# Layer 2's first product with four pairs by seven half products on weights that layer 1 stored; layer 1's half tile sooner, input sums staggered, one step of a row later

## The chip, the core and the metric

The kernel runs on one core of one Trainium2 chip. The engines that matter are TensorE (PE, matmuls; its weight loads are PEld and overlap the matmuls), VectorE (DVE), ScalarE (ACT), GpSimd (POOL, little used here) and SyncE (SP), which only issues DMAs, in the order in which they stand in its queue. The metric is the device time of one execution in microseconds (us).

## The reference

The input x has 2048 tokens of 640 channels. Two layers are computed, each a spectral block and a block that mixes tokens:

```python
for _ in range(2):
    n = layernorm(x)                                   # over the 640 channels
    x = x + irfft2(rfft2(n) * (w_r + 1j * w_i))
    h = layernorm(x)
    u = gelu(h.T @ w1 + b1)                            # over tokens: [640, 2048] @ [2048, 1728]
    x = x + (u @ w2 + b2).T                            # [640, 1728] @ [1728, 2048]
```

Both layers use the same w1, b1, w2, b2, w_r and w_i. All is float32.

## The kernel before

**Stages.** `run` calls `a0_first`, then for each layer `a1` and `a2` (spectral block) and the MLP: `b1st` for layer 1, `b2nd` for layer 2. The instructions go through a small helper (`Pin`), so that the profile puts all of them on line 57; only DMA issues keep lines of their own.

**Products.** A float32 factor is split into two fp16 parts, a high and a low one (wh and wl for weights, hh and hl for the input of the MLP, uh and ul or u for its middle). A product then is three matmuls: high x high, high x low, low x high. The split of a weight tile needs its scale: ScalarE squares and sums the raw tile (`scan1`, written to `junk`), TensorE adds the partitions with `ones`, and VectorE makes a power of two (`scale1`). ScalarE then writes the high part, VectorE the low part (`wsplit`). Weights arrive by DMA in halves of 512 KB (`wload`, tiles named raw, S, or wh and wl where a free buffer of those serves).

**First product.** Its output has 14 tiles of 128 rows of F (the last holds 64 rows, and computes its two parts side by side, so that it takes 64 matmuls in place of 16 x 2 x 3 = 96). Each matmul has 320 columns. Layer 1 takes tiles 0 to 4 and the half tile (`L` = 13) whole (`plain`), and tiles 5 to 12 as four pairs (`PD` = 4). A pair is a 2 x 2 block product by Winograd's form: seven half products in place of eight, each of 8 x 3 = 24 matmuls of 320 columns. For it the weights are combined (`form`, S1 to S4) and split anew (`hi`, `lo`, tile wo), the input too, once for all pairs: `tsum`, `thi`, `tlo` make T1 to T4 of tiles k and k + 8 of the input, four sums and two parts for each k from 0 to 7. The seven results are added up in X (named uf in layer 1) by `evict`. Layer 2 takes all 14 tiles whole, 13 x 96 + 64 = 1312 matmuls.

**Second product.** Layer 1 computes 16 rows whole; while a row runs, the start of the next spectral block (`a0_fold1`, `a0_hi` with tile fh, `a0_lo` with tile fl, `s1_all`) is done for the row before it. Layer 2 takes eight pairs by seven half products of 21 matmuls.

**What sets the order.** In `b1st` the table `SIDE` says, as (tile, step): calls, what stands before step j of a whole tile; `FORM` and `DONE` do the same in `pairs`. In `b2nd` before, `ahead` and `prep` do it. Each engine and SP's queue run strictly in the order of the program; a DMA that waits holds up those behind it. With `pin` set the order is that of the code.

**Names the change touches.** In `b1st`: `SIDE`, `plain`, `hi`, `lo`, `pairs`, the second product's `held` and `s1_all`. In `b2nd`: all of its first product. `rawtile`, `wopen` and `wload` choose the buffers of the weights.

Of the kernel before, what the change touches and what calls it, by code (L numbers as in the profile page):

```python
# [20 lines left out]
SEQ = [t + 7 * i for t in (0, 6, 1, 2, 3, 4, 5) for i in range(2)]  # L21
# [13 lines left out]
M0, PD = 5, 4  # L35
LASTW = 24
# [104 lines left out]
class Layers:  # L141
# [51 lines left out]
    def setup(self):  # L193
# [29 lines left out]
        self.xs[0] = [A["x"][j] for j in range(NJ)]  # L223
        self.xs[4] = [A["out"][j] for j in range(NJ)]
# [435 lines left out]
    def a1(self, first):  # L660
# [317 lines left out]
    def a2(self, li):  # L978
# [6 lines left out]
        self.hf = [ph.tile([128, 2, 320], F32, name=f"hf{j}_{self.n}") for j in range(NJ)]  # L985
        p = self.push("a2", side=self.sq)

        xts = [p.tile([128, 642], F32, name=f"xt{i}_{self.n}") for i in range(5)]
        for q in xts:
            G.memset(q[:, D:], 0.0)  # L990
# [47 lines left out]
        for i in range(NJ + 3):  # L1038
# [60 lines left out]
    def wtile(self, m):  # L1099

        k, i = m // NFT, m % NFT if m < NFT else m - NFT
        if self.second:
            i = i // 2 + i % 2 * NQ if k else SEQ[i]
        return min(k, 1), i, NFT if k else NJ

    def rawtile(self, m, c):

        if not self.second and m in (8, 12):
            q = self.t(self.wp[1], [128, NJ, 128], F16, "wl" if c else "wh", 1)
# [18 lines left out]
    def wopen(self, m):  # L1128
        wh, wl = (self.t(self.wp[m % 2], [128, NJ, 128], F16, a, 1) for a in ("wh", "wl"))
# [29 lines left out]
    def b1st(self, li):  # L1159
# [9 lines left out]
        self.wsplit(1, hi=False)  # L1169
        self.wload(2)  # L1170
# [75 lines left out]
        def plain(ft):  # L1246
# [43 lines left out]
        s2, c2 = (self.base.tile([128, PD], F32, name=f"{a}1") for a in ("s2", "c2"))  # L1290

# [28 lines left out]
        def lo(n):  # L1320
# [3 lines left out]
            V.scalar_tensor_tensor(w[:, 1], src[n], s2[:, d:d + 1], w[:, 0], op0=ALU.mult, op1=ALU.subtract)  # L1324

# [43 lines left out]
        def pairs():  # L1369
            for n in range(NP + 1):  # L1370
# [16 lines left out]
                if not n:  # L1387
                    self.wload(a + 1)
# [10 lines left out]
                if i == 2 and not end:  # L1399
# [30 lines left out]
        for d in range(PD - 1):  # L1430
# [9 lines left out]
            (1, 1): [(tlo, 1)],  # L1440
            (2, 0): [(tsum, 2), (thi, 2), (self.wopen, 3), (self.scan1, L)], (2, 3): [(tlo, 2)],
            (2, 6): [(self.wsplit, 3, (0,))], (2, 8): [(self.wsplit, 3, (1,)), (self.wload, 6)],
            (2, 10): [(tsum, 3), (thi, 3)], (2, 13): [(tlo, 3)],
            (3, 0): [(tsum, 4), (thi, 4), (self.wopen, 4)], (3, 2): [(self.wsplit, 4, (0,))],
            (3, 4): [(self.wsplit, 4, (1,)), (self.wload, 7), (tlo, 4)], (3, 7): [(tsum, 5), (thi, 5)],
            (3, 6): [(self.scan1, 5)], (3, 11): [(tlo, 5)],
# [659 lines left out]
```

## Time and profile before

| | |
|---|---|
| time, median of 3 runs | 1002.23 us (1001.63 to 1249.45) |
| the profiled execution, its own time | 1001.94 us |
| its span | 1000.2 us |
| granted TensorE clock | 0.998 |
| TensorE busy | 963.3 us (96%), 8873 matmuls |
| VectorE busy | 731.3 us (73%) |
| ScalarE busy | 590.2 us (59%) |
| GpSimd busy | 253.9 us (25%) |
| SP's DMA queue | 134.35 MB, 40.7% of the 16 DMA engines |

The span runs from the first instruction to the last, and the execution's time adds what lies around it. In the views, `out<-in` names what an instruction writes and reads, `[0.66 <-DVE wo]` says that the engine was idle for 0.66 us until VectorE's write of wo released it, and x2 that two instructions stand in one row. In the views of windows each engine has its busy time in the window, and behind it the count of its instructions; the last three columns are the granted clock as a share of 2.4 GHz, the busy share of the 16 DMA engines and the bytes moved in GB/s. TensorE's matmuls overlap in their rows, so that a row's time is longer than the distance between two starts.

### The profile page before, as it was taken

What the parts mean: (1) busy time and instruction counts of PE and PEld (TensorE: products, weight loads), DVE (VectorE), ACT (ScalarE), POOL (GpSimd) and SP (SyncE); (2) the same over time, 40 slices, a digit from 0 to 9 for tenths busy, and PEclk for the clock granted to TensorE, in tenths of its full rate; (3) what the DMA queues carried; (4) which work ended last, traced back from release to release, by engine and by line L of the source; (5) the groups of instructions that cost most, each with busy time, mean ns of one, the idle gap of its engine ahead of it and who ended that gap; (6) DMA issues with size and microseconds to landing.
All of it is one profiled execution on the core that took longest, in us unless ns stands there. A gap on an engine that the chain in (4) does not pass through costs nothing. (4 is left out here: it accounts for less than half of the span.)

```text
span 1000.2 us, 21980 instructions
## 1 busy us (share of the span) xinstructions
PE 963.3 (96%) x8873; PEld 707.5 (71%) x8873; DVE 731.3 (73%) x1416; ACT 590.2 (59%) x919; POOL 253.9 (25%) x409
## 2 busy tenths in 40 slices
PE   5899999999899999999998999999999999999998
PEld 4678666777677767777777786667777777777776
DVE  7989677966878877777765896784533635878885
ACT  6978699655777765555532777964433435344431
POOL 7759786000000011111121896830000000000000
PEclk9999999999999999999999999999999999999999
DMA  9773475321321653333224633735322322455411
GB/s 326 251 222 111 136 243 170 119 91 47 104 85 53 211 174 127 127 127 126 96 89 156 192 95 103 235 130 210 110 70 76 110 75 98 146 166 176 146 45 53
DMA packets 53861, 135.74 MB, mean 136 GB/s; under 512 B 6376, under 2 KB 11392, under 8 KB 53760
## 3 DMA queue, kind: packets, MB, share of 16 engines
q1 hardware_dynamic: 53760, 134.35, 40.7%
q8 instruction: 69, 1.13, 0.4%
q14 instruction: 32, 0.26, 0.1%
HBM read 111.25 MB, written 23.07 MB: 134 GB/s over the span
## 5 line engine op out<-in xcount | busy, mean ns | idle before, releaser
L57 PEld LDWEIGHTS <-wh 128*128 128x128 f16 x2480 | 240.6, 98 | 95.0 <-issue 3.1
L57 PE MATMUL ps<-hf,wh 128*128 128x320 f16 x864 | 179.0, 299 | 0.0
L57 PEld LDWEIGHTS <-wl 128*128 128x128 f16 x1360 | 133.0, 98 | 51.8
L57 PEld LDWEIGHTS <-wo 128*128 128x128 f16 x1176 | 114.5, 98 | 47.8 <-DVE wo L57 2.5
L57 DVE SCALAR_TENSOR_TENSOR wl<-raw,s,wh 128x1024 f16<-128x1024 f32 (+2 forms) x72 | 87.9, 1245 | 68.6 <-ACT wh L57 68.0
L57 PE MATMUL ps<-hf,wl 128*128 128x320 f16 x448 | 133.1, 299 | 0.0
L57 PE MATMUL ps<-hh,wh 128*128 128x320 f16 x640 | 130.8, 299 | 1.6 <-ACT hh L57 1.6
L57 PE MATMUL ps<-hl,wh 128*128 128x320 f16 x640 | 129.0, 299 | 0.0
L57 ACT ACTIVATE wh<-raw,s 128x1024 f16<-128x1024 f32 (+2 forms) x74 | 74.6, 1036 | 73.4 <-PE ps L57 65.4
L57 PE MATMUL ps<-hh,wl 128*128 128x320 f16 x576 | 115.8, 299 | 0.0
L57 PE MATMUL ps<-u,wo 128*128 128x320 f16 x504 | 69.9, 299 | 0.0
L57 DVE TENSOR_TENSOR xt<-xt,ps 128x320 f32<-128x320 f32 (+1 forms) x96 | 45.0, 490 | 30.6 <-ACT ec L57 20.3
L57 POOL TENSOR_TENSOR r<-v,mh 128x1 f32<-128x1 f32 (+1 forms) x56 | 33.6, 601 | 123.3 <-DVE nm L57 111.4
L57 DVE BATCH_NORM_STATS2 st<-xt 128x6 f32<-128x320 f32 x128 | 56.2, 480 | 3.1 <-DMA xt<-x 2.5
L57 ACT ACTIVATE junk<-raw 128x896 bf16<-128x896 f32 (+1 forms) x54 | 53.3, 986 | 5.1 <-DMA raw<-w 4.2
L57 PE MATMUL ps<-hf,wo 128*128 128x320 f16 x384 | 53.2, 299 | 0.9 <-DVE wo L57 0.9
L57 PE MATMUL ps<-tDi,yh 128*128 128x322 f16 x240 | 50.2, 299 | 0.0
L57 PE MATMUL ps<-u,wh 128*128 128x320 f16 x336 | 48.4, 299 | 0.0
L57 PE MATMUL ps<-u,wl 128*128 128x320 f16 x336 | 48.2, 299 | 0.0
L57 PE MATMUL ps<-tm,F 128*128 128x128 f32 (+1 forms) x256 | 30.1, 312 | 15.1 <-ACT tm L57 12.2
L57 POOL MEMSET hf<- 64x640 f16 x1 | 0.8, 775 | 168.8 <-DVE hf L57 168.8
L57 PE MATMUL ps<-tD,s1h 128*128 128x160 f16 (+1 forms) x320 | 42.0, 234 | 1.2 <-ACT s1h L57 0.9
(208 smaller groups left out, 1975.9 us busy)
## 6 DMA issues: line engine op xcount, KB each, us to landing
xt<-x SPq DMA_DIRECT2D x80, 320.0 KB, 3.2
raw<-w SPq DMA_DIRECT2D x50, 512.0 KB, 3.7
x<-xt SPq DMA_DIRECT2D x48, 320.0 KB, 2.2
raw<-w SPq DMA_DIRECT2D x32, 448.0 KB, 3.2
raw<-w2z SPq DMA_DIRECT2D x32, 448.0 KB, 3.3
w<-w SPq DMA_DIRECT2D x44, 321.0 KB, 3.0
out<-xt SPq DMA_DIRECT2D x15, 320.0 KB
stk<-rest SPq DMA_DIRECT2D x36, 64.0 KB, 3.5
```

Source lines behind the costliest of these rows:

```text
L57: i = f(*a, **k)
```

## The change

1. Layer 2's first product takes tiles 0 to 4 and 13 whole (`SINGLE`) and tiles 5 to 12 as four pairs by seven half products, as layer 1 does: 5 x 96 + 64 + 28 x 24 = 1216 matmuls.
2. Its weights are not built again. Layer 1 stores the fp16 parts of its whole tiles (`wput`, 11 transfers of 512 KB into `ws`) and of the 28 half products (28 of 512 KB into `wos`, in `lo`) in DRAM, and layer 2 loads them (`wget`, `wfetch`). Layer 2's raw loads, scales, high and low parts of w1 fall away, in a2 and in b2nd; the input sums `tsum`, `thi`, `tlo` and the evictions of half products come in.
3. In layer 1 the half tile is computed before tile 4, the sums are spread over the tiles from tile 1 on, tile 8 of w1 is loaded sooner, the scans of tiles 7 and 8 and the first pair's weights move, and the order of TensorE is that of the code from tile 2 on.
4. In layer 1's second product the folded products of row 1 (`s1_all(1)`) move from step 25 of row 2 to step 12 of row 3.
5. In layer 2's second product the formed weights lie in other buffers (`seven`), with the same instructions; loads of w2 are issued at other places.

```diff
+SINGLE = *range(M0), NFT - 1
@@ setup
+        self.ws = {m: self.dram.tile([128, 2, NJ, 128], F16, name=f"ws{m}") for m in SINGLE}
+        self.wos = [self.dram.tile([128, 2, 8, 128], F16, name=f"wos{n}") for n in range(7 * PD)]
@@ a1, a2
-            add(("wl",), "SP", .8, [("S", 0)], 9, lambda: (self.wload(0), self.wopen(0)), lag=3)
-        for q in range(4):
+            add(("wl",), "SP", .8, [("S", 0)], 9, lambda: self.wget(0), lag=3)
+        for q in range(4 * first):
...
-                self.wload(1)
-            if 3 < i < 8:
+                self.wload(1) if first else self.wget(1)
+            if first and 3 < i < 8:
                 self.wsplit(0, self.quarter(i - 4)[0], hi=False, part=self.quarter(i - 4)[1])
@@
+    def wput(self, m):
+        for i in range(1 if m == NFT - 1 else 2):
+            self.tc.keep_in_program_order(self.nc.sync.dma_start(self.ws[m][:, i], self.w[m][i]))
+
+    def wget(self, m):
+        self.wopen(m)
+        for i in range(1 if SINGLE[m] == NFT - 1 else 2):
+            self.nc.sync.dma_start(self.w[m][i], self.ws[SINGLE[m]][:, i])
@@ b1st
         self.wsplit(1, hi=False)
+        for k in range(2):
+            self.wput(k)
         self.wload(2)
...
             V.scalar_tensor_tensor(w[:, 1], src[n], s2[:, d:d + 1], w[:, 0], op0=ALU.mult, op1=ALU.subtract)
+            self.tc.keep_in_program_order(nc.sync.dma_start(self.wos[n], w))
...
-            (4, 0): [(tsum, 6), (thi, 6), (self.wopen, L)], (4, 2): [(self.wsplit, L, (0,))],
-            (4, 4): [(self.wsplit, L, (1,)), (tlo, 6)], (4, 7): [(tsum, 7), (thi, 7)],
-            (4, 6): [(self.scan1, 6)], (4, 10): [(tlo, 7)],
-            (L, 0): [(hi, 0), (lo, 0), (hi, 1)], (L, 2): [(lo, 1), (form, 3)], (L, 5): [(form, 4), (form, 2)], (L, 9): [(hi, 2), (lo, 2)],
-            (L, 8): [(self.scan1, 7)],
...
+            (L, 6): [(tlo, 7)],
+            (4, 0): [(self.wload, 8), (hi, 0), (lo, 0), (hi, 1)], (4, 2): [(lo, 1), (form, 3), (self.scan1, 7)], (4, 3): [(form, 4), (form, 2)],
+            (4, 6): [(hi, 2), (lo, 2), (self.scan1, 8)],
...
-        for ft in (*range(M0), L):
+        for ft in (*range(M0 - 1), L, M0 - 1):
+            self.pin = "rest" if ft < 2 else True
             plain(ft)
...
-                if i == (23 if last else 25) and j > 1:
+                if i == (23 if last else 25) and j > 2:
                     self.s1_all(j - 1, *f)
-                if i == 25 and j == 1:
-                    held = f
-                if i == 18 and j == 2:
-                    self.s1_all(0, *held)
+                if i == 25 and j in (1, 2):
+                    held[j - 1] = f
+                if (i, j) in ((18, 2), (12, 3)):
+                    self.s1_all(j - 2, *held[j - 2])
@@ b2nd, first product: the input sums, the whole tiles
+        SIDE = {
+            (1, 1): [(tsum, 0), (thi, 0)], (1, 4): [(tsum, 1), (thi, 1), (tlo, 0)], (1, 10): [(tlo, 1)],
+            **{(2 + k // 2, k % 2 * 8): [(tsum, k + 2), (thi, k + 2)] for k in range(6)},
+            **{(2 + k // 2, k % 2 * 8 + 3): [(tlo, k + 2)] for k in range(6)},
+        }
...
+            if m + 2 < NS:
+                self.wget(m + 2)
+            else:
+                for n in (2, 3) if m == NS - 2 else (4, 5):
+                    wfetch(n)
@@ b2nd, the pairs
+        for n in range(NP + 1):
+            if n < NP:
+                bank[n] = self.big()
+                first_product(n)
+                wfetch(n + 6)
+            if n:
+                first_evict(n - 1)
...
+        for b in (M0 + 2 * PD - 2,):
+            y = held[LATE]
+            gelu(b, x[:, 1], x[:, 1])
+            usum(1, x[:, 1], fs[:, 0])
+            usum(2, x[:, 1], y[:, 1])
+            usum(3, x[:, 0], fs[:, 1])
+            uhi(LATE, 1, 2, x)
+            ulo(LATE, 1, 2, x)
+            uhi(LATE, 4, 3, fs[:, 1:])
+            ulo(LATE, 4, 3, fs[:, 1:])
```

Three places show what moves. The first is SP's queue at the start of layer 1's MLP, behind the last store of x (raw are the halves of w1's tile 2, S those of the half tile, the later raw those of tiles 5 and 6). Before:

```order
L1062 DMA x_15_102<-xt_296_2556 128x640
L1124 DMA raw_3385<-w 128x1024
L1124 DMA raw_3387<-w 128x1024
L1124 DMA S_3457<-w 128x1024
L1124 DMA S_3459<-w 128x1024
L1124 DMA raw_3658<-w 128x1024
L1124 DMA raw_3660<-w 128x1024
L1124 DMA raw_3778<-w 128x1024
```

After (ws_135 to ws_137 are the stored parts of tiles 0 to 2):

```order
L1067 DMA x_15_102<-xt_296_2575 128x640
L1128 DMA ws_136<-wh_2752 128x2048
L1141 DMA raw_3408<-w 128x1024
L1128 DMA ws_136<-wl_2753 128x2048
L1141 DMA raw_3410<-w 128x1024
L1141 DMA S_3480<-w 128x1024
L1141 DMA S_3482<-w 128x1024
L1128 DMA ws_137<-wh_3675 128x2048
L1128 DMA ws_137<-wl_3676 128x2048
L1141 DMA raw_3683<-w 128x1024
L1141 DMA raw_3685<-w 128x1024
```

The high part of tile 1 now is stored ahead of tile 2's two loads, and its low part between them.

The second is ScalarE at the start of layer 1's pairs (wo are the high parts of the half products' weights, junk the scans, uf 64x640 the half tile's swap). Before:

```order
L57 ACTIVATE wo_4111<-raw_3658,s_3461 128x1024
L57 ACTIVATE wo_4114<-raw_3660,s_3461 128x1024
L57 ACTIVATE junk,sq_4155<-raw_3882 128x1024
L57 ACTIVATE junk,sq_4155<-raw_3884 128x1024
L57 ACTIVATE wo_4162<-S_4141,s_3461 128x1024
L57 ACTIVATE uf_500_3439<-ps_4110 64x640 x2
L57 ACTIVATE up_500_3445<-uf_500_3439,b1s,c_76 128x640
L57 ACTIVATE wo_4226<-S_4125,s_3461 128x1024
L57 ACTIVATE uf_500_3436<-ps_4197,c_3462 128x320 x2
L57 ACTIVATE wo_4255<-S_4139,s_3461 128x1024
L57 ACTIVATE wo_4286<-S_4258,s_3461 128x1024
L57 ACTIVATE junk,sq_4289<-wh_4222 128x1024
```

After:

```order
L57 ACTIVATE uf_500_3459<-ps_4009 64x640 x2
L57 ACTIVATE up_500_3468<-uf_500_3459,b1s,c_76 128x640
L57 ACTIVATE wo_4116<-raw_3683,s_3484 128x1024
L57 ACTIVATE wo_4120<-raw_3685,s_3484 128x1024
L57 ACTIVATE junk,sq_4138<-raw_4018 128x1024
L57 ACTIVATE junk,sq_4138<-raw_4020 128x1024
L57 ACTIVATE wo_4169<-S_4149,s_3484 128x1024
L57 ACTIVATE junk,sq_4173<-wh_4112 128x1024
L57 ACTIVATE junk,sq_4173<-wl_4114 128x1024
L57 ACTIVATE up_500_3467<-ps_4111,b1s,c_76 128x640
L57 ACTIVATE wo_4262<-S_4136,s_3484 128x1024
L57 ACTIVATE uf_500_3459<-ps_4237,c_3485 128x320 x2
```

The swap of the half tile, its gelu and all scans of tile 8 (junk of wh and wl) now stand ahead of the fourth wo; before, the scans of tile 8 stood behind the sixth.

The third is VectorE at the end of layer 2's first product and the start of its second (u are the low parts of the middle, ux and f its values, us and fs their sums, xt the output). Before:

```order
L57 TENSOR_TENSOR fs_11960<-f_11959,fs_11960 128x320
L57 TENSOR_TENSOR fs_11960<-f_11959 128x320
L57 TENSOR_TENSOR fs_11960<-f_11959,fs_11960 128x320
L57 SCALAR_TENSOR_TENSOR u_1328_10489<-fs_11960,su,u_1328_10489 128x640
L57 SCALAR_TENSOR_TENSOR u_1328_10489<-f_11959,su,u_1328_10489 128x640
L57 SCALAR_TENSOR_TENSOR u_1328_10489<-fs_11960,su,u_1328_10489 128x320
L57 SCALAR_TENSOR_TENSOR xt_12101<-ps_12106,cp,xt_12101 128x320
L57 TENSOR_TENSOR S_1429_12158<-raw_11616,S_1418_12015 128x896
L57 SCALAR_TENSOR_TENSOR xt_12101<-ps_12131,cp,xt_12101 128x2x320
L57 SCALAR_TENSOR_TENSOR wl_12156<-raw_11616,sp,wl_12156 128x896
```

After:

```order
L57 TENSOR_TENSOR us_10519<-u_1323_10511 128x320
L57 SCALAR_TENSOR_TENSOR hf_9650<-hf_9650,sp 128x896
L57 SCALAR_TENSOR_TENSOR ux_1324_10518<-ps_12023,c_3485,ux_1324_10518 128x320
L57 TENSOR_TENSOR us_10519<-ux_1324_10518,us_10519 128x320
L57 TENSOR_TENSOR us_10519<-ux_1324_10518,u_1323_10511 128x320
L57 TENSOR_TENSOR us_10519<-ux_1324_10518,us_10519 128x320
L57 SCALAR_TENSOR_TENSOR u_1323_10511<-ux_1324_10518,su,u_1323_10511 128x640
L57 SCALAR_TENSOR_TENSOR u_1323_10511<-us_10519,su,u_1323_10511 128x960
L57 SCALAR_TENSOR_TENSOR xt_12079<-ps_12084,cp,xt_12079 128x320
L57 TENSOR_TENSOR hf_9650<-raw_11181,hf_9650 128x896
L57 SCALAR_TENSOR_TENSOR xt_12079<-ps_12109,cp,xt_12079 128x2x320
L57 SCALAR_TENSOR_TENSOR hf_9650<-raw_11181,sp,hf_9650 128x896
```

Ahead of the first eviction into xt there now stand, besides the three sums and the low parts, a low part of the weights (hf) and the last eviction of the first product (ux<-ps).

## Rows read from the trace of the kernel before

**Rows 1.** The page: span, busy time of each engine

```profile
span 1000.2 us, 21980 instructions
PE 963.3 (96%) x8873; PEld 707.5 (71%) x8873; DVE 731.3 (73%) x1416; ACT 590.2 (59%) x919; POOL 253.9 (25%) x409
```

**Rows 2.** Chain of waits, its last long piece: start, us, what

```profile
664.44 332.32 PE ps L57 x2444
```

**Rows 3.** Windows of 50 us, layer 2's first product

```profile
700.00:750.00 50.00, 50.00 (x370) 36.02 (x369) 22.08 (x29) 20.26 (x25) 0.00 (x0) 1.00 0.28 89
```

**Rows 4.** VectorE's groups by form, 665 to 1000 us: busy, mean ns, idle before

```profile
L57 DVE SCALAR_TENSOR_TENSOR wl<-raw,sp,wl 128x896 f16<-128x896 f32 x16 | 18.3, 1144 | 0.0
...
L57 DVE SCALAR_TENSOR_TENSOR xt<-ps,cp,xt 128x320 f32<-128x320 f32 x32 | 17.6, 551 | 22.8 <-ACT m L57 13.5 <-PE ps L57 9.2
...
L57 DVE SCALAR_TENSOR_TENSOR u<-fs,su,u 128x960 f16<-128x960 f32 x6 | 7.3, 1218 | 1.8 <-ACT u L57 1.8
...
L57 DVE TENSOR_TENSOR fs<-f 128x320 f32<-128x320 f32 x14 | 6.8, 485 | 4.8 <-ACT f L57 4.8
...
L57 DVE SCALAR_TENSOR_TENSOR u<-f,su,u 128x640 f16<-128x640 f32 x7 | 6.1, 878 | 0.0
```

**Rows 5.** The page's DMA issues: raw loads, median us to landing

```profile
raw<-w SPq DMA_DIRECT2D x50, 512.0 KB, 3.7
```

**Rows 6.** Timeline of TensorE at the end of layer 2's a2

```profile
660.85 3.32 PE L57 MATMUL ps<-hh,wh 128*128 128x320 f16 x23 [0.54 <-ACT hh L57]
664.44 0.70 PE L57 MATMUL ps<-hh,wh 128*128 128x320 f16 x4 [0.27 <-ACT hh L57]
```

**Rows 7.** Timeline of VectorE and TensorE, layer 2's second product starts

```profile
844.76 1.14 DVE L57 SCALAR_TENSOR_TENSOR wl<-raw,sp,wl 128x896 f16<-128x896 f32 x1
...
836.84 8.31 PE L57 MATMUL ps<-u,wo 128*128 128x320 f16 x60
...
848.25 1.93 PE L57 MATMUL ps<-u,wl 128*128 128x320 f16 x13
```

**Rows 8.** Windows of 5 us, layer 1's first product

```profile
230.00:235.00 5.00, 4.76 (x40) 3.42 (x38) 3.17 (x4) 4.74 (x9) 0.00 (x0) 1.00 0.00 0
250.00:255.00 5.00, 4.06 (x29) 2.43 (x27) 2.83 (x3) 4.09 (x7) 0.00 (x0) 1.00 0.26 95
255.00:260.00 5.00, 3.35 (x25) 2.39 (x26) 5.00 (x6) 4.35 (x8) 0.00 (x0) 1.00 0.44 125
260.00:265.00 5.00, 4.88 (x37) 3.54 (x37) 4.66 (x18) 3.19 (x5) 0.00 (x0) 1.00 0.25 90
```

**Rows 9.** Timeline of TensorE, start of layer 1's pairs

```profile
255.57 3.16 PE L57 MATMUL ps<-hf,wo 128*128 128x320 f16 x22 [0.85 <-DVE wo L57]
...
260.12 0.16 PE L57 MATMUL ps<-sq,ones 128*128 128x1 bf16 x1 [1.02 <-ACT junk L57]
```

**Rows 10.** Timeline of TensorE, row 2 of layer 1's second product

```profile
372.92 0.28 PE L57 MATMUL ps<-tM,fh 128*128 128x128 f16 x2 [0.90 <-ACT fh L57]
373.78 0.23 PE L57 MATMUL ps<-tM,fl 128*128 128x128 f16 x1 [0.57 <-DVE fl L57]
```

**Rows 11.** Timeline: SP issues tile 8, ScalarE scans it

```profile
243.73 0.33 SPq L1124 DMA_DIRECT2D wh<-w  x1
...
257.74 1.04 ACT L57 ACTIVATE junk<-wh 128x1024 bf16<-128x1024 f32 x1
```

**Rows 12.** Timeline of ScalarE, start of layer 1's MLP

```profile
182.61 1.06 ACT L57 ACTIVATE junk<-raw 128x1024 bf16<-128x1024 f32 x1 [3.49 <-DMA raw<-w]
```

**Rows 13.** Timeline of VectorE and TensorE, tile 2 of layer 1 starts

```profile
194.23 2.48 DVE L57 SCALAR_TENSOR_TENSOR wl<-raw,s,wh 128x1024 f16<-128x1024 f32 x2 [1.05 <-ACT wh L57]
...
195.74 0.43 PE L57 MATMUL ps<-hh,wl 128*128 128x320 f16 x2
```

**Rows 14.** Windows of 5 us with heavy DMA traffic

```profile
175.00:180.00 5.00, 5.00 (x38) 3.45 (x37) 5.00 (x8) 3.39 (x6) 0.00 (x0) 1.00 0.74 224
...
340.00:345.00 5.00, 5.00 (x39) 3.59 (x38) 4.90 (x9) 5.00 (x8) 0.78 (x1) 1.00 0.93 343
```

More of the change, by code (lines that the diff above doesn't have):

```diff
@@ L984, in a2 @@
         ph = self.push("hf", side=self.sp)
-        self.hf = [ph.tile([128, 2, 320], F32, name=f"hf{j}_{self.n}") for j in range(NJ)]
+        self.hfs = ph.tile([128, NJ, 2, 320], F32, name=f"hf{self.n}")
+        self.hf = [self.hfs[:, j] for j in range(NJ)]
         p = self.push("a2", side=self.sq)
         xts = [p.tile([128, 642], F32, name=f"xt{i}_{self.n}") for i in range(5)]
+        if not first:
+            self.among = 1
         for q in xts:
@@ L1128, in wopen @@
     def wopen(self, m):
-        wh, wl = (self.t(self.wp[m % 2], [128, NJ, 128], F16, a, 1) for a in ("wh", "wl"))
+        turn = m + (not self.second and m in (M0 - 1, NFT - 1))
+        wh, wl = (self.t(self.wp[turn % 2], [128, NJ, 128], F16, a, 1) for a in ("wh", "wl"))
         self.w[m] = wh, wl
@@ L1398, in pairs @@
                     self.scan1(a)
-                if i == 2 and not end:
+                if i == 2 and d and not end:
                     self.scan1(a + 1)
@@ L1637, in b2nd @@
-        places = [(px, f"wo{i}") for i in range(3)] + [(q, a) for q in self.wp for a in ("wh", "wl")]
-        src, wo = {}, {}
-        def raw(d, a):
-            return self.wraws[NFT + 2 * d + int(a[1]) - 1][int(a[2]) - 1]
-        def form(n):
+        X = [p.tile([128, 2, 2, 320], F32, name=f"ux{d}_{self.n}") for d in range(2)]
+        fs = p.tile([128, 4, 320], F32, name=f"us{self.n}")
+        four = [q.bitcast(F16).rearrange("p a (b c) -> p (a b) c", c=320) for q in self.hf]
+        flat = self.hfs.rearrange("p j a c -> p (j a c)")
@@ L1733, in b2nd @@
                 run = both(m, ps, self.w.pop(m))
-                ahead(m)
-            steps = prep(m)
             for j in run:
-                if m and j in ((1, 2) if m == 1 else (6, 8) if m == 2 else (2, 4)):
-                    next(steps)
+                for f, *a in SIDE.get((m, j), ()):
+                    f(*a)
                 if j == 10:
@@ L1770, in b2nd, with operand @@
-        self.usums(f, fs, "T2", "T3")
-        self.usums(f, fs, "T4")
-        uhi(t, 4, 2, fs[:, 1:3])
-        uhi(t, 1, 2, x)
-        uhi(t, 6, 1, fs[:, 3:4])
-        ulo(t, 4, 2, fs[:, 1:3])
-        ulo(t, 1, 2, x)
-        ulo(t, 6, 1, fs[:, 3:4])
-        LATE = t
+            gelu(ft, held[t], pv, c1)
+            if not dup(m):
+                later.append(lambda t=t: upper(t, held[t]))
+        self.pin = True
+        for m in range(NFT, NFT + 3):
+            self.wload(m)
+        def operand(b, j):
+            if b[0] == "T":
+                return tuple(four[j + i][:, int(b[1]) - 1] for i in (0, 8))
+            return tuple(self.h[j + 8 * (b[1] == "2")][i][:, int(b[2]) - 1] for i in range(2))
@@ new lines, in done @@
+        def done(f, d):
+            t, x = f % 7, X[d % 2][:, (f - M0) % 2]
+            if f < NFT // 2 - 1:
+                gelu(f, held[t], x)
+                return lambda: upper(t, held[t])
+            gelu(f, x, x)
+            if f < NFT // 2:
+                return lambda: (upper(t, x), lower(t, x, held[t]))
+            return lambda: lower(t, held[t], x)
+        DONE = {7 * d + 4 + 2 * i: M0 + 2 * d + (i if d < PD - 1 else 1 - i) for d in range(PD) for i in range(2)}
+        first_ops, first_n = ops, NP
@@ new lines, in b2nd @@
+        FIRST = {
+            2: [(form, 0), (hi, 0), (form, 1)], 3: [(lo, 0), (hi, 1)], 4: [(lo, 1), (form, 2), (form, 3), (hi, 2)],
+            5: [(lo, 2), (hi, 3)], 6: [(lo, 3)],
+        }
+        later = []
+        for n in range(NP + 1):
[5 more added lines that the diff above has]
+                first_evict(n - 1)
+            for a in later:
+                a()
+            later = []
+            if n - 1 in DONE:
+                f = DONE[n - 1]
+                if n < NP:
+                    later.append(done(f, ops[n - 1][0]))
+            if n == NP - 1:
+                for a in later:
+                    a()
+                later = []
+                x, f = X[(PD - 1) % 2][:, 0], M0 + 2 * PD - 2
+                LATE = f % 7
+                usum(0, held[LATE][:, 1], held[LATE][:, 0])
+            if n == NP - 1:
+                gelu(f, x[:, 0], x[:, 0])
+            if n >= NP - 7:
+                for g, *a in FIRST.get(n - NP + 7, ()):
+                    g(*a)
```

258 lines of the change are left out of this document (152 added, 106 removed).

## Prediction

> **What bounds the kernel now.** First the page: TensorE is busy 963.3 us of a span of 1000.2 us, VectorE 731.3, ScalarE 590.2 [rows 1]. So nearly all of the time is matmuls, and a change can do only two things of weight: take matmuls away, or close the 36.9 us in which TensorE idles. The reader should then look at the chain that ended last, to see whether the matmuls touched here lie on it: from 664.44 us on it is one unbroken piece of TensorE, 332.32 us with 2444 matmuls, the whole MLP of layer 2 [rows 2]. One matmul of 320 columns takes 332.32 / 2444 = 0.136 us there, and a window of 50 us from its middle has TensorE at 50.00, VectorE at 22.08 and ScalarE at 20.26 [rows 3]. So layer 2's MLP is worth exactly its number of matmuls, as long as nothing new waits, and the two other engines have over half of their time free for what the change gives them. Last come windows of 5 us around layer 1's MLP, where TensorE is not full; they price the other two parts.
>
> **Layer 2's first product.** Before: 13 whole tiles of 96 matmuls and the half tile of 64, 1312 in all. After: 5 x 96 + 64 + 28 half products of 8 x 3 = 24, that is 480 + 64 + 672 = 1216. So 96 fewer: 96 x 0.136 = **-13.06 us** (with 0.136 the matmul of the piece above). The half products have the same 320 columns as the matmuls priced, so no other price is needed.
>
> What pays for it on other engines: the input sums (per k four sums of 0.49 us [rows 4] on VectorE and a low part, eight times, in the single tiles) and the evictions of 28 half products, 30 instructions on VectorE and 16 on ScalarE of 0.55 us [rows 4] or near. Both lie in stretches in which VectorE was busy 44% [rows 3]; the scaling and splitting of w1 (two instructions on each of the two engines a tile) goes away in return. I cost them at nothing, except at the seam below. If that cover were gone, VectorE alone would have to work more than 13.06 us a single tile or 3.26 us a half product, and by these rows it has about half of that.
>
> The weights now come as fp16 parts from DRAM, 28 + 11 transfers of 512 KB in place of 28 raw ones, so 39 / 28 of the bytes in this stretch, where DMA was busy 0.28 of the time [rows 3]. A raw load of that size lands 3.7 us after its issue [rows 5]. Nearly all fetches are issued a tile or five half products (16 us) before use. Tightest is tile 2's high part: its buffer is that of tile 0, whose last use lies 32 matmuls before tile 2, 32 x 0.136 = 4.35 us against 3.7. I take 0 here (0 to 1).
>
> **The end of layer 2's a2**, where TensorE waits 0.54 + 0.27 us for ScalarE's hh [rows 6]. Two weight splits leave ScalarE there, but their place in the order goes partly to other hh. I take 0 (-0.5 to +0.5).
>
> **The seam to the second product of layer 2.** Before, the low part for product 4 ends at 844.76 + 1.14 = 845.90 and TensorE takes it at 848.25 [rows 7]: 2.35 us of room, counted from TensorE's start of the second product at 836.84. After, VectorE arrives late. From the end of half product 25, 6.53 us before that start, it has two evictions, a sum, a low part, another eviction, four sums, u parts of 640 and 960, a sum, a low part and the last eviction: by [rows 4] 2 x 0.55 + 0.49 + 1.14 + 0.55 + 4 x 0.49 + 0.88 + 1.22 + 0.49 + 1.14 + 0.55 = 9.5 us. That ends about 3.2 us after the start. The last gelu (I take 0.6 for its 320 columns), three sums, and the u part of 960, which first waits for ScalarE's high part of about the same length, follow: 3.2 + 0.6 + 1.5 + 1.2 + 1.2 = 7.7 us. This u part is needed after 78 matmuls, 10.6 us, so it holds nothing up. Behind it stand evictions of 0.55 and 0.88, a form of at most 1.14 and the low part of 1.14: 11.4 us, where the low part is needed at 848.25 - 836.84 = 11.41. So the room of 2.35 us is used up to zero. Bounds: 0 if VectorE overlaps the ends of its instructions as in [rows 7], 2.5 if each hand-over between the engines costs some tenths more. I take **+0.5**, near the lower bound, as the sum itself comes out at the edge.
>
> **Layer 1, start of the pairs.** TensorE is busy only 4.06 + 3.35 + 4.88 of 15 us from 250 to 265, and 4.76 from 230 to 235 [rows 8]: 2.71 + 0.24 = 2.95 us idle. The gaps end with VectorE's wo (0.85) and with ScalarE's junk, the scan of a weight tile (1.02) [rows 9]: forming the first pair's weights and the scans of tile 8 come too late, because the half tile that covers them lasts only 64 matmuls, 8.7 us, and input sums are still in the queues beside it. After, the last tile before the pairs is a whole one (13.06 us), the sums are finished before, and the order has all scans of tile 8 ahead of the fourth half product's weights. I take all of it, **-2.95 us** (bounds 0 and -2.95).
>
> **Layer 1, the row step.** The folded row's products at row 2 wait 0.90 for fh and 0.57 for fl [rows 10]. At row 3, step 12, 15 steps of three matmuls or 6 us later, fh and fl are long ready, and ScalarE and VectorE have the parts of row 3 ahead of the extra evictions in their queues, so nothing is late in turn: 0.90 + 0.57 = **-1.47 us** (bounds 0 to 0.5 given back at row 3's own step).
>
> **Layer 1, the stores.** 11 + 28 new transfers enter SP's queue between the raw loads; SP waits at each until its part is written, and the loads behind it wait too. In the pairs a raw load has time: the pieces of tile 8 were issued at 243.73 and scanned at 257.74 [rows 11], 14.0 us against 3.7 to land. At the start of the MLP it has none. Raw loads for tile 2 and the half tile go out together; ScalarE waited 3.49 us for the second of them, until 182.61 [rows 12]. Now the store of tile 1's high part stands ahead of both, that of its low part between them. From the second load the chain goes over scans, the first T high part and the scale to tile 2's low part, which starts at 194.23 with two of 1.24 us, so the first half is done at 195.47; TensorE uses it at 195.74 [rows 13]. Room: 0.27 us at the end, and about 0.9 us in idles on the way. The DMA engines moved 224 GB/s just there [rows 14]; two more transfers of 0.524 MB at that rate are 4.7 us, of which perhaps half falls ahead of the second load: 2 us late, less 1.2 of room = **+0.8** (bounds 0 and 4.7 - 1.2 = 3.5).
>
> **Sum**, against the profiled execution's 1001.94 us: 1001.94 - 13.06 - 2.95 - 1.47 + 0.8 + 0.5 = 985.76. The median of the runs shown is 0.29 higher, so 986.0 us.
>
> **A rule that speaks against it.** The row above has loads back to back at 224 GB/s, with the engines 0.74 busy; another stretch has 343 GB/s at 0.93 [rows 14]. The Trainium skill, page "DMA: Bandwidth & Descriptors", section Bandwidth (Measured), gives 341 GB/s for transfers of 1 MB and 425 GB/s for 16 MB, and says that transfers should be batched to 1 MiB or more; a kernel that adds 39 stores of half that size would do the opposite. By the page's 341 the stores of a pair are hidden and the sum stays; by the row's 224 they are not quite, which is the second rival.
>
> **Rivals.**
> 1. *Several small waits take the gain's edge.* The bounds above all on their bad side: +3.5 at tile 2, +2.5 at the seam, 1 at layer 2's tile 2, 0.5 twice, and half of the 2.95 not won: 985.8 + 2.7 + 2.0 + 1 + 1 + 1.5 = 994.0. For it: room at the two places is near zero. Against: they are independent, all must go wrong. Chance 0.15, times of 990 to 1000.
> 2. *The stores starve layer 1's pairs, slower than before.* A pair needs 4 raw loads and 7 stores, 11 x 0.524 = 5.77 MB, in 168 x 0.136 = 22.8 us: 253 GB/s. At 343 it is hidden; at 224 a pair takes 25.8 us, 2.9 us behind each, 11.7 us in four, which the lead of 14.0 - 3.7 = 10.3 us nearly swallows. To eat the gain of 16.2 us too the lag must reach 26.5 us, 6.6 a pair: 5.77 MB in 29.4 us, below 196 GB/s it ends slower than before. At 180 GB/s: 32.1 us a pair, 37 us behind, 985.8 + 37.2 - 10.3 = 1012.7. Against it: TensorE, ScalarE and VectorE don't wait for a DMA anywhere in these pairs now, and 343 GB/s were reached beside a full TensorE (5.00 of 5 us [rows 14]). Chance 0.04.
> 3. *More is won than counted.* The two new waits don't come, the hh waits go: 985.8 - 1.3 - 0.8 = 983.7, and further where shorter queues on ScalarE shorten a2: 981 to 983. Chance 0.06.
>
> **How the numbers follow.** My forecast has 0.75, with a range of its own of 983 to 990. Two per cent, 20 us, is about what a measurement of this kernel can tell from no change. The saving is 1.6%, so the forecast lies inside that: faster by over 2% means below 982.2, half of rival 3 and little of the rest, 0.04; slower by over 2%, above 1022.3, only a part of rival 2, 0.01; the rest 0.95. For the range I leave out the upper part of rival 1 above 992, rival 2 and the far half of rival 3: 982.5 to 992.
>
> **What would show it.** In the profile after: layer 2's MLP one piece of about 2348 matmuls and 319.3 us; windows at 5.00 from tile 2 of layer 1 through the pairs; no waits for fh and fl at row 2; a wait of TensorE for wl of about 0.8 us at layer 1's tile 2; and one of about 0.5 us for the low part of product 4 behind the seam. The prediction is wrong where TensorE waits for a DMA in a single tile or a pair, or where VectorE has a backlog over more than a seam.

## The result and the profile after

The changed kernel takes 983.34 us (median of 4 runs, 982.91 to 984.71), the kernel before 1002.05 us beside it: a ratio of 0.982 with a 95% interval of 0.9805 to 0.9836, or 18.7 us less. That lies in the predicted range (982.5 to 992) and 2.7 us below the predicted 986.0. By the bound of 2% it counts as no change, which had the chance 0.95, though the interval is clear of 1. The profiled execution took 984.71 us with a span of 982.6 us; it is the slowest of the four; the first line of the table below has 1.3 us of that.

The page after, its span, its busy times and its traffic:

```profile
span 982.6 us, 21924 instructions
PE 950.5 (97%) x8777; PEld 698.7 (71%) x8777; DVE 739.7 (75%) x1462; ACT 577.7 (59%) x910; POOL 253.4 (26%) x409
...
q1 hardware_dynamic: 60960, 160.56, 49.1%
...
HBM read 117.02 MB, written 43.52 MB: 163 GB/s over the span
```

Against [rows 1] TensorE has 8873 - 8777 = 96 matmuls less, and it is busy 12.8 us less. VectorE has 8.4 us more, ScalarE 12.5 less. The 20 MB written more are the stores of layer 1.

Where the time went can be read without any model: up to layer 2's MLP both kernels have the same number of matmuls, so the start of the same matmul (counted from the first) is compared in both traces, and the stretches of layer 2 by their own first and last.

| stretch | before, us | after, us | change | predicted |
|---|---|---|---|---|
| start to the first matmul of layer 1's MLP | 167.66 | 168.96 | +1.30 | 0 |
| layer 1, first product | 171.03 | 167.26 | -3.77 | -2.95 + 0.8 |
| layer 1, second product, its first 433 matmuls | 56.07 | 54.27 | -1.80 | -1.47 |
| rest of it and layer 2's spectral block | 262.55 | 262.49 | -0.06 | 0 |
| layer 2, first product | 179.54 | 166.07 | -13.47 | -13.06 |
| layer 2, second product | 159.60 | 159.93 | +0.33 | +0.5 |
| behind the last matmul's start | 3.72 | 3.59 | -0.13 | 0 |

The first line is no part of the change, as far as the traces show: of its 1.30 us, 1.1 are there within the first 200 matmuls, and the other profiled kernels below reach this place at 167.75 to 168.70. Without it the parts give -18.9 us, near the -18.7 of the medians; with it they give -17.6, as the two spans do. The fourth line is not exact to tenths either: in the kernels below, which leave this stretch alone, it takes 260.76 to 263.25 us. The lines that the change touches repeat better: kernels with the same code there agree within 0.2 us, tile 2 of layer 1 apart (below).

The stretches that were not full before are full now, and layer 2's first product still is. Windows of 50 us, and of 5 us in layer 1's pairs (columns as in [rows 3] and [rows 8]):

```profile
200.00:250.00 50.00, 50.00 (x375) 36.05 (x374) 37.64 (x75) 35.34 (x47) 0.00 (x0) 1.00 0.49 171
250.00:300.00 50.00, 50.00 (x376) 36.08 (x375) 41.15 (x69) 32.01 (x43) 0.00 (x0) 1.00 0.73 255
300.00:350.00 50.00, 50.00 (x379) 36.06 (x377) 43.85 (x83) 36.05 (x51) 0.78 (x1) 1.00 0.70 248
350.00:400.00 50.00, 50.00 (x412) 36.80 (x410) 38.94 (x109) 32.04 (x47) 8.84 (x23) 1.00 0.42 144
...
700.00:750.00 50.00, 50.00 (x370) 36.02 (x369) 8.81 (x17) 10.21 (x16) 0.00 (x0) 1.00 0.35 114
750.00:800.00 50.00, 50.00 (x370) 36.02 (x369) 24.99 (x45) 16.68 (x24) 0.00 (x0) 1.00 0.48 160
...
255.00:260.00 5.00, 5.00 (x43) 3.63 (x41) 2.66 (x15) 1.61 (x3) 0.00 (x0) 1.00 0.91 295
...
270.00:275.00 5.00, 5.00 (x39) 3.60 (x37) 3.13 (x5) 4.97 (x9) 0.00 (x0) 1.00 0.97 397
```

TensorE is at 50.00 where the pairs start, against the gaps of [rows 8]; the DMA engines move about 250 GB/s on the mean of the pairs and 397 GB/s at a peak, with TensorE at 5.00 beside it. The chain of waits after, its two long pieces (start, us, what):

```profile
659.46 156.52 PE ps L57 x1151
...
831.06 148.25 PE ps L57 x1090
```

The single piece of [rows 2] is now two with the seam between them, from 816 to 831 us, where the chain goes over VectorE and ScalarE. TensorE itself loses 0.33 us there. Timeline of the seam after (all engines, start, us, what, idle before and its releaser):

```profile
824.76 6.14 PE L57 MATMUL ps<-u,hf 128*128 128x320 f16 x44
...
825.61 1.53 ACT L57 ACTIVATE xt<-xt,b2s 128x640 f32<-128x640 f32 x2
...
827.59 0.55 DVE L57 SCALAR_TENSOR_TENSOR xt<-ps,cp,xt 128x320 f32<-128x320 f32 x1 [0.63 <-ACT m L57]
...
829.85 1.14 DVE L57 SCALAR_TENSOR_TENSOR hf<-raw,sp,hf 128x896 f16<-128x896 f32 x1
...
831.06 2.21 PE L57 MATMUL ps<-u,hf 128*128 128x320 f16 x15 [0.16 <-DVE hf L57]
```

The low part for product 4 ends at 829.85 + 1.14 = 830.99, 11.93 us after the start of the second product at 819.06; before it was 9.06 us after it [rows 7]. TensorE starts product 4 at 11.41 in both kernels and stops before its third matmul, behind 21 + 21 + 44 = 86 matmuls: it needed the low part at 11.68 and went on at 12.00.

### The profile page after: what moved, and what is told of

It is laid out like the page before. It is cut to its first block, busy times and chain, and to the rows that moved or that the text cites. A ratio compares the mean times of both kernels' runs of the same rounds, so it can differ in the third digit from the quotient of the medians.

```text
span 982.6 us, 21924 instructions
## 1 busy us (share of the span) xinstructions
PE 950.5 (97%) x8777; PEld 698.7 (71%) x8777; DVE 739.7 (75%) x1462; ACT 577.7 (59%) x910; POOL 253.4 (26%) x409
## 3 DMA queue, kind: packets, MB, share of 16 engines
q8 instruction: 69, 1.13, 0.5%
## 5 line engine op out<-in xcount | busy, mean ns | idle before, releaser
L57 PEld LDWEIGHTS <-wh 128*128 128x128 f16 x2184 | 211.6, 98 | 83.2 <-issue 2.5
L57 PE MATMUL ps<-hf,wl 128*128 128x320 f16 x592 | 153.6, 299 | 0.0
L57 PE MATMUL ps<-hh,wh 128*128 128x320 f16 x464 | 92.0, 299 | 1.3 <-ACT hh L57 1.3
L57 PE MATMUL ps<-hl,wh 128*128 128x320 f16 x424 | 85.4, 299 | 0.0
L57 PEld LDWEIGHTS <-wo 128*128 128x128 f16 x672 | 65.4, 98 | 25.2
L57 PE MATMUL ps<-hh,wl 128*128 128x320 f16 x368 | 70.4, 299 | 0.0
L57 PE MATMUL ps<-u,hf 128*128 128x320 f16 x504 | 69.9, 299 | 0.2 <-DVE hf L57 0.2
L57 PEld LDWEIGHTS <-hf 128*128 128x128 f16 x504 | 49.2, 98 | 19.6 <-DVE hf L57 0.5
L57 DVE SCALAR_TENSOR_TENSOR wl<-raw,s,wh 128x896 f16<-128x896 f32 (+2 forms) x44 | 54.3, 1270 | 3.8 <-ACT wh L57 3.8
L57 ACT ACTIVATE wh<-raw,s 128x896 f16<-128x896 f32 (+2 forms) x44 | 43.3, 1023 | 11.1 <-DVE s L57 6.8
```

What stands on the lines that cost most here:

```text
L57: i = f(*a, **k)
```

## The experiments

In all of them the comparison is with the kernel before on the same chip and, stretch by stretch, by the starts of the same matmuls as above. The medians of the kernel before were 1001.56 us beside the first four and 1000.96 us beside the last three, 0.5 and 1.1 us below the 1002.05 beside the changed kernel. So a distance between the medians of two changed kernels is sure to about 1 us at best, and what a step costs is read from the stretches.

**What a wait of TensorE costs: the row step undone.**

```diff
-                if i == (23 if last else 25) and j > 2:
+                if i == (23 if last else 25) and j > 1:
                     self.s1_all(j - 1, *f)
-                if i == 25 and j in (1, 2):
+                if i == 25 and j == 1:
                     held[j - 1] = f
-                if (i, j) in ((18, 2), (12, 3)):
+                if (i, j) == (18, 2):
```

> The changed kernel with one thing undone: the folded products of row 1 go back from step 12 of row 3 to step 25 of row 2. Theory A: a wait of TensorE costs the idle time that its row shows and, on top, the 0.299 - 0.136 = 0.163 us by which a matmul's row is longer than the step to the next one, since the overlap is lost at each wait. Two waits of 0.90 and 0.57 come back: +1.80 us between the same matmuls of layer 1's second product, total about 985.1. Rival B: a wait costs what its row shows, +1.47 us, total about 984.8, and the rest of the gain in this stretch came from elsewhere. The trace tells them apart: the same matmul, counted from the start, stands 1.8 or 1.5 us later.

983.85 us, ratio 0.9822 (0.9806 to 0.9838). Timeline of TensorE at row 2:

```profile
368.07 0.30 PE L57 MATMUL ps<-hf,wl 128*128 128x320 f16 x1
368.98 0.28 PE L57 MATMUL ps<-tM,fh 128*128 128x128 f16 x2 [0.61 <-ACT fh L57]
369.84 0.23 PE L57 MATMUL ps<-tM,fl 128*128 128x128 f16 x1 [0.57 <-DVE fl L57]
```

Both waits are back, though the first is 0.61 and not 0.90 as in [rows 10]. The stretch takes 55.78 us against 54.27 in the changed kernel: 1.51 us for waits that show 0.61 + 0.57 = 1.18. The rows say why: the matmul at 368.07 lasts 0.30 us, and without a wait the next would have started 0.136 us after it, at 368.21; it starts at 368.98, so 0.77 are lost where 0.61 are shown. Twice 0.163 on top of 1.18 is 1.51 (for the second wait it is a row of 128 columns, 0.219 us long where the next would start after 0.056, with the same difference). That is theory A in its mechanism, at a smaller wait than either theory took. The total moved by 0.5 us, too little to tell anything by itself.

**Layer 1's first product in its old order, with the stores.** `SIDE`, the order of the tiles and the buffers as in the kernel before, `wput` behind each tile's split (two places of the edit; the others move buffers, loads, scans and scales to where they were):

```diff
-            (4, 0): [(self.wload, 8), (hi, 0), (lo, 0), (hi, 1)], (4, 2): [(lo, 1), (form, 3), (self.scan1, 7)], (4, 3): [(form, 4), (form, 2)],
-            (4, 6): [(hi, 2), (lo, 2), (self.scan1, 8)],
...
+            (L, 0): [(hi, 0), (lo, 0), (hi, 1)], (L, 2): [(lo, 1), (form, 3)], (L, 5): [(form, 4), (form, 2)], (L, 9): [(hi, 2), (lo, 2)],
+            (L, 8): [(self.scan1, 7)],
...
-        for ft in (*range(M0 - 1), L, M0 - 1):
-            self.pin = "rest" if ft < 2 else True
+        for ft in (*range(M0), L):
             plain(ft)
```

> The changed kernel with layer 1's first product in its old order (half tile after tile 4, old places of the input sums, of the load of tile 8, of scans and of the first pair's weights), the stores kept. Theory A: the five waits of before come back (0.24, 0.66, 0.85, 0.17 and 1.02, together 2.94 us), each with 0.163 us on top: +3.76 us in that stretch, total about 987.1. Rival B: +2.94 us alone, total 986.3. Rival C: the old order with the stores in SP's queue waits longer than the old order without, over 4.5 us, because loads come later: total above 987.8.

987.18 us, ratio 0.9855 (0.9841 to 0.987): 3.84 us above the changed kernel. Timeline of TensorE, its waits in this stretch:

```profile
235.28 0.16 PE L57 MATMUL ps<-sq,ones 128*128 128x1 bf16 x1 [0.31 <-ACT junk L57]
...
244.13 0.30 PE L57 MATMUL ps<-hl,wo 128*128 128x320 f16 x1
244.38 0.45 PE L57 MATMUL ps<-hh,wo 128*128 128x320 f16 x2
...
251.73 0.45 PE L57 MATMUL ps<-hh,wo 128*128 128x320 f16 x2 [0.66 <-DVE wo L57]
...
256.01 3.16 PE L57 MATMUL ps<-hf,wo 128*128 128x320 f16 x22 [0.85 <-DVE wo L57]
...
259.01 0.19 PE L57 MATMUL ps<-sq,ones 128*128 128x1 bf16 x2
259.37 0.17 PE L57 MATMUL ps<-sq,ones 128*128 128x1 bf16 x1 [0.16 <-ACT junk L57]
260.55 0.16 PE L57 MATMUL ps<-sq,ones 128*128 128x1 bf16 x1 [1.02 <-ACT junk L57]
```

The five waits of before are back near their old lengths, 3.00 us together, and the stretch is 171.10 us against 167.26, 3.84 longer. Read from start to start, the five cost 0.45, 0.82, 1.01, 0.30 and 1.16, 3.74 in all. The surplus is 0.163 only at the two that stand behind a matmul of 320 columns; behind a `ones` it is 0.138, since that row lasts 0.163 us and the next starts 0.025 after it. A sixth place shows no idle at all: at 244.38 a matmul starts 0.25 us after the one ahead, in place of 0.136, which is 0.12 lost inside the overlap. 3.74 + 0.12 = 3.86. So theory A in its mechanism, and neither the shown idle alone (B) nor waits of over 4.5 us by the stores (C); that its 5 x 0.163 came so near is partly luck, as it had 0.07 too much and left out 0.12. (The profiled execution, 985.78 us, was only 1.1 us above the changed kernel's, because stretches that the edit does not touch were shorter in it.)

**Layer 2's part alone**, with both edits above undone together:

> The changed kernel with both changes of layer 1's order undone (row step and first product), so that only layer 2's first product, its loads and layer 1's stores are left of the change. Theory: parts add up, +3.76 + 1.80 = 5.6 us against the changed kernel, total about 988.9, 13.1 us below the kernel before; layer 2's first product from its first matmul to the first of the second product stays at 166.1 us (179.5 before, 13.06 for 96 matmuls and 0.4 for shorter waits for hh). Rival: the orders help each other, and the sum is off by over 1 us.

987.82 us (987.07 to 989.39), ratio 0.9865 (0.9851 to 0.988), 13.7 us below the kernel before. In the trace layer 1's first product has 171.19 us (+3.93), the row step's stretch 55.76 (+1.49), and layer 2's first product 166.07, as in the changed kernel. So the parts add up, 5.4 us in the trace for 5.6 expected, with the row step smaller than expected as in the first experiment. The medians differ by 4.5 us, and their runs spread over 2.3 us; the difference of 0.9 is not resolved.

**The stores alone**, added to the kernel before; nothing reads them:

```diff
         self.wsplit(1, hi=False)
+        for k in range(2):
+            self.wput(k)
         self.wload(2)
...
             V.scalar_tensor_tensor(w[:, 1], src[n], s2[:, d:d + 1], w[:, 0], op0=ALU.mult, op1=ALU.subtract)
+            self.tc.keep_in_program_order(nc.sync.dma_start(self.wos[n], w))
...
```

> The kernel before with nothing but layer 1's 39 stores added; nothing reads them. Theory: they are hidden, the pairs stay at 0.136 us a matmul with about 255 GB/s moved, and tile 2 starts without a wait since the second raw load comes about 1 us later and the idles of ScalarE take that up: 0 us, total about 1002. Rival (the prediction's term): tile 2's low part comes 0.8 us late, and waits in the old order of the pairs grow with late scans: +1 to +3 us, total 1003 to 1005.

1001.96 us against 1001.56, ratio 1.0004 (0.9995 to 1.0013). TensorE's timeline at tile 2 and a window over the pairs:

```profile
195.57 0.43 PE L57 MATMUL ps<-hl,wh 128*128 128x320 f16 x2
196.46 0.44 PE L57 MATMUL ps<-hh,wl 128*128 128x320 f16 x2 [0.45 <-DVE wl L57]
```

```profile
247.00:340.00 93.00, 90.31 (x676) 64.62 (x674) 77.46 (x135) 64.30 (x89) 0.00 (x0) 1.00 0.70 249
```

In the pairs nothing is lost: the 2.69 us of idle there are the four old waits at their start. But tile 2 does wait, 0.45 us shown, 0.61 with the lost overlap, and the wait of 0.24 for a scan behind it became 0.39: the first product is 171.79 us against 171.03. A shorter wait for fh at row 2 (0.56 for 0.90) gives 0.33 back. Both theories are half right: hidden in the pairs, not at tile 2.

**Room at tile 2: two more stores between its two raw loads**, in the changed kernel:

```diff
...
         for k in range(2):
             self.wput(k)
+        for i in range(2):
+            self.tc.keep_in_program_order(self.nc.sync.dma_start(self.spare[i], self.w[1][i]))
         self.wload(2)
```

> The changed kernel with two more stores of 512 KB (tile 1's parts again, into a buffer that nothing reads) in SP's queue between the two raw loads of layer 1's tile 2. Theory: the two stores of the changed kernel made the second load 1.1 us late, ScalarE's and VectorE's idles took up 1.0 of that and 0.16 us of room are left; two more make it another 1 to 2.4 us late (2.4 at 437 GB/s for the two, less where they share), so TensorE waits for wl at the start of tile 2, 0.9 to 2.3 us plus 0.163: total 984 to 986. Rival: the load's time is not set by the stores beside it, and nothing waits: 983.3.

985.39 us, ratio 0.9838 (0.9822 to 0.9855), 2.05 above the changed kernel. ScalarE's wait for the second raw load, first in the changed kernel, then here:

```profile
185.04 1.06 ACT L57 ACTIVATE junk<-raw 128x1024 bf16<-128x1024 f32 x1 [3.78 <-DMA raw<-w]
```

```profile
186.14 1.06 ACT L57 ACTIVATE junk<-raw 128x1024 bf16<-128x1024 f32 x1 [6.01 <-DMA raw<-w]
...
196.79 0.45 PE L57 MATMUL ps<-hh,wh 128*128 128x320 f16 x2 [1.12 <-ACT wh L57]
...
198.11 0.45 PE L57 MATMUL ps<-hh,wl 128*128 128x320 f16 x2 [0.60 <-DVE wl L57]
```

Counted from the first matmul of the MLP, this scan starts after 14.95 us before the change (182.61 [rows 12] less 167.66), 16.08 after it (185.04 - 168.96), and 18.17 here (186.14 - 167.97): 2.09 us more for two stores. Of these 2.09, 1.31 are a later issue (SP issues the load 9.91 us after the MLP's start, 8.60 in the changed kernel), the other 0.78 a later landing. TensorE waits 1.12 + 0.60, and the first product grows by 2.10 us (169.36): 1.72 shown, 0.138 and 0.163 give 2.02. So the theory holds, and the changed kernel stands at the edge of its room there. No run here shows the 437 GB/s of the expectation's upper bound; the highest rate over 5 us is about 420.

Seven kernels, this one left out, have the changed kernel's queue at this place, and in all of them SP issues the load 8.6 us after the MLP's start. The scan came after 15.80 (row step undone), 16.03 to 16.12 (four kernels, with them the changed one), 16.68 (the next experiment) and 16.74 (the stores alone). TensorE waited only in the last two, 0.39 and 0.45 us shown. It is the landing that varies, by 0.9 us, and that decides between no wait and 0.6 us; why it varies is not shown.

**The stores of the pairs twice**, in the changed kernel:

```diff
...
             self.tc.keep_in_program_order(nc.sync.dma_start(self.wos[n], w))
+            self.tc.keep_in_program_order(nc.sync.dma_start(self.spare[n], w))
```

> The changed kernel with each of the 28 stores of half product weights in layer 1 made twice, the second into a buffer that nothing reads. A pair then moves 18 x 0.524 = 9.44 MB in 22.8 us, 414 GB/s, above any row of before. Theory: the DMA engines carry up to about 370 to 400 GB/s, a pair falls 1 to 2.7 us behind, 4 to 11 in four, and the lead of about 10 us of the raw loads takes that: TensorE loses 0 to 3 us, total 983 to 986. Rival (the bound of the prediction's second rival): they carry 224 GB/s as in the row of 175 to 180 us, a pair takes 42 us, TensorE loses over 60 us, total above 1040.

985.86 us, ratio 0.9847 (0.983 to 0.9863), 2.5 above the changed kernel. Windows over the pairs, and TensorE's timeline behind them:

```profile
247.00:336.00 89.00, 89.00 (x669) 64.18 (x668) 71.93 (x129) 59.46 (x83) 0.00 (x0) 1.00 0.97 376
...
275.00:280.00 5.00, 5.00 (x39) 3.62 (x37) 3.77 (x4) 4.94 (x8) 0.00 (x0) 1.00 1.03 419
```

```profile
359.33 0.16 PE L57 MATMUL ps<-sq,ones 128*128 128x1 bf16 x1 [0.24 <-ACT junk L57]
360.40 0.16 PE L57 MATMUL ps<-sq,ones 128*128 128x1 bf16 x1 [0.91 <-ACT junk L57]
```

The DMA engines carry 376 GB/s over 89 us, and in the pairs TensorE loses nothing, 89.00 of 89. The bill comes where the traffic ends: rows of x and w2 for the second product land late, ScalarE waits 2.36 us for x at 349.52, and TensorE waits for scans. In that stretch, the second product's first 433 matmuls, 1.6 us are lost. Another 0.6 is lost at tile 2 (the wait of 0.39 for wl); that stands ahead of all the doubled stores and is the varying landing, not their price. So the theory holds in the pairs, though it did not say where the bill would come, and the 224 GB/s by which the prediction priced its second rival are far below what the engines carry.

**The seam without its wait**, the first two bias additions on GpSimd:

```diff
-                    T.activation(row(d, i), row(d, i), AF.Identity, bias=self.b2[:, d + NQ * i:d + NQ * i + 1])
+                    if d:
+                        T.activation(row(d, i), row(d, i), AF.Identity, bias=self.b2[:, d + NQ * i:d + NQ * i + 1])
+                    else:
+                        self.G.tensor_scalar(row(d, i), row(d, i), self.b2[:, d + NQ * i:d + NQ * i + 1], None, op0=ADD)
```

> The changed kernel with one thing moved: the two bias additions to the first rows of x in layer 2's second product (1.53 us on ScalarE, between the last u part and the first eviction) go to GpSimd, which has nothing to do there. Theory: at the seam VectorE waits 0.63 us for ScalarE's copy m, which stands behind these additions; without them the low part for product 4 is 0.6 us earlier, and TensorE's wait of 0.16 us (0.33 with the lost overlap) is gone: 159.93 us of the second product become 159.60, total about 983.0. Rival: the low part is held by VectorE's own queue, and the 0.33 us stay.

983.11 us, ratio 0.9817 (0.9803 to 0.9832). The seam in this kernel:

```profile
819.25 4.39 POOL L57 TENSOR_SCALAR xt<-xt,b2s 128x640 f32<-128x640 f32 x2 [160.71 <-DMA xt<-x]
...
820.01 1.60 DVE L57 SCALAR_TENSOR_TENSOR hf<-hf,sp 128x896 f16<-128x896 f32 x1
...
828.55 1.14 DVE L57 SCALAR_TENSOR_TENSOR hf<-raw,sp,hf 128x896 f16<-128x896 f32 x1
```

```profile
823.72 8.51 PE L57 MATMUL ps<-u,hf 128*128 128x320 f16 x61
```

TensorE's row of 61 matmuls runs through the place where the changed kernel's broke off at 831.06, and the second product takes 159.67 us in place of 159.93, near the 159.60 of before. VectorE's wait of 0.63 for m is gone, so the wait was ScalarE's queue, not VectorE's length alone. But the low part comes 828.55 + 1.14 - 818.02 = 11.67 us after the start of the second product, 0.26 sooner and not the 0.6 expected, and TensorE still loses 0.05 us there, hidden in the overlap of its rows. What is missing went lost on VectorE: while GpSimd was at the two additions, an instruction that takes 1.14 us in the changed kernel, and in its fifteen other places in this one, took 1.60. Whether GpSimd's work is the cause, no run here tells. The total of 983.11 can't be told from 983.34.

## Why the prediction was right, and where its terms were off

**What bounds the kernel, and the main term.** The reading of [rows 2, 3] held: in layer 2 the matmuls alone set the time, and nothing that was given to VectorE, ScalarE or the DMA engines came to the surface, but for 0.33 us at the seam. 13.06 us were predicted, 13.47 measured, and every kernel here with this product has 166.06 to 166.08 us for it. The rest of 0.4 is the end of a2, which had been put at 0 within 0.5. TensorE's timeline there after the change:

```profile
656.53 2.69 PE L57 MATMUL ps<-hh,wh 128*128 128x320 f16 x18 [0.26 <-ACT hh L57]
659.46 0.43 PE L57 MATMUL ps<-hh,wh 128*128 128x320 f16 x2 [0.24 <-ACT hh L57]
```

0.54 + 0.27 [rows 6] became 0.26 + 0.24, 0.31 us less. The last 0.1 stands in starts that show no idle: three matmuls here started 0.17 to 0.22 us after the one ahead before the change, 0.21 lost together, and one does after it, 0.09. That ScalarE's two weight splits left this place is the likely cause, but no run had them back alone. Tile 2 of layer 2 waits for nothing, as taken.

**The gaps of layer 1: right in place, too small by one step.** The prediction took each gap at the idle time of its row or window, 2.95 and 1.47 us. All of them closed, but they gave 3.77 and 1.80. The step that was too small is taking the idle of a window, 15 - (4.06 + 3.35 + 4.88) = 2.71, for the loss: busy time counts the whole of the last matmul ahead of a wait, 0.299 us, of which only 0.136 would have passed before the next started. Read from start to start, the two waits at row 2 cost 1.06 + 0.74 = 1.80, and the five at the pairs 3.68, with 0.12 more where a late start shows no idle: 3.80 against the 3.77 measured. Undoing each part shows the same surplus at waits of other lengths. That is 1.1 of the 2.7 us between prediction and median.

**Tile 2 of layer 1: the mechanism right, the size off.** +0.8 was taken from a second load 2 us late and 1.2 us of room. It came 1.13 us late, 0.62 of it because SP issued it later (8.60 us after the MLP's start for 7.98) and 0.51 by its landing; the idles of ScalarE and VectorE and the 0.27 us at the end took that up. Timeline after, VectorE and TensorE, to compare with [rows 13]:

```profile
195.66 2.48 DVE L57 SCALAR_TENSOR_TENSOR wl<-raw,s,wh 128x1024 f16<-128x1024 f32 x2 [1.04 <-ACT wh L57]
```

```profile
197.06 0.43 PE L57 MATMUL ps<-hh,wl 128*128 128x320 f16 x2
```

The first half is ready at 195.66 + 1.24 = 196.90, 0.16 us before TensorE wants it. The stores alone in the old order, where the load was 1.79 us late, gave a loss near the predicted one (0.61 us), and two more stores gave 2.1. So the 0.8 was a case that two of the seven traces with this queue do show, and the lateness, 0.85 to 1.79 us in them for the 2 assumed, is the mis-sized number. That the changed kernel's trace has no wait here is luck of the landing.

**The seam.** The backlog was worked out to 11.4 us where 11.41 were wanted, with +0.5 for the hand-overs; the low part came at 11.93, and the price was 0.33 (0.16 shown). Several things in the sum were off. Its 9.5 us from 6.53 ahead of the start end 3.0 us behind it, not 3.2; the trace has 3.6 there, and the u part of 960 ends at 7.9 for the 7.7 worked out. VectorE's wait of 0.63 after that for the copy m, behind two bias additions on ScalarE, was not in it; taking the additions away took this wait away. And the evictions, the form and the low part behind that took 3.4 us for the 3.7 counted, as their rows overlap. The need was read 0.27 too early: 11.41 is where product 4 starts, its low part is first read two matmuls later, at 11.68. So an arrival half a microsecond later than worked out cost a third, and that the term of +0.5 came near is partly luck.

**The rivals.** The first did not come: of its waits only the seam's was there. The second, starved pairs, was priced by the wrong row: the 224 GB/s of [rows 14] are a window in which the engines were busy 0.74 of the time, not a limit. The kernel before had a higher rate elsewhere:

```profile
10.00:15.00 5.00, 4.13 (x30) 3.06 (x29) 4.90 (x12) 3.91 (x8) 4.43 (x6) 1.00 1.05 401
```

Under a longer queue the engines moved 376 GB/s over 89 us. The Trainium skill, page "DMA: Bandwidth & Descriptors", section Bandwidth, Measured, gives 425 GB/s for transfers of 16 MB, for loads issued from GpSimd, with the rule to batch to 1 MiB or more. Here loads and stores of 512 KB, issued from SP with several queued, reached 419 GB/s over 5 us: the trace agrees with that rate, at half the size that the rule names. The third rival, more than counted, is what happened in part. Tile 2's wait did not come, the seam's was smaller and the waits for hh shrank, about 1.4 us together, by its own mechanism; the other 1.1 us are the surplus at each wait, which it did not have.

**The row step** stays without a price at row 3, as taken: no idle shows there, and the 0.15 us hidden in one late start were 0.13 before.

**The signs.** The windows at 5.00 and the missing waits at row 2 came as named. Layer 2's MLP was to be one piece of the chain and is two, the wait at layer 1's tile 2 did not come, and the one behind the seam was 0.33 for 0.5. Nowhere in a single tile or a pair did TensorE wait for a DMA.

## What to carry to other kernels

When a pipelined engine's wait is to be removed, price it from the start of the instruction ahead to the start of the one behind, less the normal distance, and not by the idle time that the row shows: here 0.14 to 0.16 us a wait, about a fifth of what closing the gaps gave. Compare starts also where no idle shows: a late start can hide inside the overlap of the rows. In an ordered queue, price added transfers by where they stand ahead of a transfer that someone waits for; here the 28 behind that place cost nothing, and twice as many cost 1.6 us, at the next stage's first loads. At a seam, follow each hand-over between the engines through both queues: here the wait came from the other engine's small bias additions.

## What was not expected of the hardware

- TensorE lost more at each wait than the idle shown, by the length of the row ahead less its normal distance to the next start: 0.163 us behind matmuls of 320 columns (0.299 less 0.136) and of 128 (0.219 less 0.056), 0.138 behind the `ones` (0.163 less 0.025), at seven waits of 0.16 to 1.02 us in two kernels.
- The 16 DMA engines held 376 GB/s over 89 us with loads and stores of 512 KB mixed, at a TensorE that stayed 89.00 us busy.
- The same load, issued 8.6 us after the same matmul behind the same transfers, was scanned 15.80 to 16.74 us after it in seven kernels, a spread of 0.9 us.
- Two bias additions of 640 columns took 4.39 us on GpSimd and 1.53 us on ScalarE. A VectorE instruction beside them took 1.60 us for its usual 1.14; the cause is not shown.
